# A fused RWKV, gated-attention and channel-mix kernel: stacked key halves for single heads, a weight split off TensorE, small steps on ScalarE, and another order

## The chip, the cores and the metric

The kernel runs on one core of one Trainium2 chip. Its time is the device time of one execution in microseconds (us); before the change the median of three runs is 636.58 us (636.41 to 636.62). A core has TensorE (PE in the profile, its weight loads PEld), VectorE (DVE), ScalarE (ACT), GpSimd (POOL) and SyncE (SP), which issues the DMAs. Each engine runs its own list of instructions in order, and the lists meet only at semaphores.

## The reference

Three layers in a row over 4 batches of 768 tokens, 384 wide, all in float32. Cut to what matters:

```python
# 1. RWKV recurrence, 8 heads of 48
y[t] = r[t] @ (state + outer(u * k[t], v[t]))
state = w[t][:, None] * state + outer(k[t], v[t])
# 2. four experts, each a causal attention with heads of 64; the two best experts of a token count
for e in range(4):
    q, k, v = x @ wq[e], x @ wk[e], x @ wv[e]
    a = softmax(where(causal, -1e9, (q @ k.T) / 8))
    out += gate[:, :, e] * (a @ v @ wo[e])
# 3. channel mix
out = x + relu(layernorm(x) * g_ln @ w_ch1) @ w_ch2
```

`wq` and `wk` are scaled by about 27, so that the scores are large and the products need more than float16.

## The kernel before

**Precision.** Matrices that TensorE multiplies are split into two float16 parts, a high one and a low one (value minus high). A product is three passes: high by high, high by low, low by high (`passes`, in the code a list of pairs). The split is made twice over in this kernel: ScalarE writes the high part (`q_hi`, `s_hi`, `hi`), then VectorE or, for weights, TensorE and ScalarE write the low part (`q_lo`, `s_lo`, `less` and `lo`).

**Stages.** A batch is 6 chunks of 128 tokens. `rwkv_chunk` computes the recurrence of a chunk by scans on VectorE and small float32 products on TensorE; its output goes transposed into the tiles `xT`, one for two chunks, five of them in turn (`SIZES`). `project` multiplies `xT` by the weights of queries and keys (`mm_q`, L1119; 12 results of a batch, each split by `q_hi` L1133 and `q_lo` L1139) and of values and gates (`mm_v`, L1175). `attend` goes over the 6 blocks of 128 queries: scores (`mm_s`, L1289, with a mask product at L1292), maximum (`s_max`, L1302 or L1307 and L1310), exponential (`s_exp`, L1325), split, transposing DMA, product with the values (`mm_av`, L1368), normalisation (`a_den`, L1381 to L1383), output projection (`mm_o`, L1416). Two blocks give 256 rows for `norm` and `mlp`: `mm_1` (L1509, 108 matmuls of 256 columns) and `mm_2` (L1542, 72 matmuls of 384 columns), 12 times in all.

**Scores.** A head has 64 rows, so queries and keys of an even head lie in rows 0 to 63 and those of an odd head in rows 64 to 127. Blocks 0 to 3 take two or four heads in one unit, and their 64-row matmuls of an even and an odd head run side by side. Blocks 4 and 5 (640 and 768 keys) take one head at a time (`alone`): 2 blocks, 4 heads and 4 batches make 32 such units. For these, four DMAs (`stack_q`, L1153) write a tile `xq` with the high part of the queries in one half of the rows and the low part in the other, and four (`stack_k`, L1161) a tile `xk` with the high part of the keys in both halves. One 128-row pass over `xq` and `xk` gives high by high plus low by high; a second, 64-row pass over `qs` and `kd` gives high by low. Each pass is two matmuls, of 512 columns and of the rest; the mask product of 128 columns and 128 rows closes the unit.

**Channel-mix weights.** `w1` and `w2` come as 12 parts of 384 columns each, `w2` in six loads of two parts. VectorE decodes a load (L501 to L503), ScalarE sums its squares (`top`, L571), and once the common scale is known TensorE multiplies a part by a diagonal of it (`times`, L651, float32), ScalarE takes the high part (L655), TensorE subtracts it in PSUM (`less`, L659) and ScalarE takes the rest (`lo`, L663). The loads of `w2` use the two slots of the ring `xnT`, which `top` frees; later the same slots hold the transposed input of `mm_1` (`n_tr`, L1481).

**Order.** A list scheduler (`Plan`) writes the instruction order of all engines when the kernel is built: at each step it takes, among the operations that could begin first, the one with the lowest due time; the due times are the table `PLACE` and `PRM`, and the operations' assumed durations stand in the decorators. The same scheduler places idle matmuls (`spin`) at the start.

Of the kernel before, what the change touches and what calls it, by code (L numbers as in the profile page):

```python
# [10 lines left out]
F16 = mybir.dt.float16  # L11
# [9 lines left out]
P = 128  # L21
# [16 lines left out]
PRM = dict(LOOK=0.0, LATE=47934.0429, UNTIL=42.7413, SPAN=5.8951, LEAST=0.3045, GAP=2.3171, LAND=3.0218, NPA=6, NCB=8, DIRECT=(), NST=10)  # L38
PLACE = {
# [21 lines left out]
    ('o', 3, 5): -870797.51, ('proj', 0): -59357.09, ('proj', 0, 's'): -132504.36, ('proj', 0, 1): 75985.76,  # L61
    ('proj', 0, 2): 89300.14, ('proj', 1): -94741.02, ('proj', 1, 1): -141865.08, ('proj', 1, 2): -157811.48,
    ('proj', 2): -48176.78, ('proj', 2, 1): 94543.45, ('proj', 2, 2): -181961.13, ('proj', 3): 107540.27,
# [12 lines left out]
    ('vals', 0, 1): 39151.57, ('vals', 0, 2): -75195.63, ('vals', 1): -80560.85, ('vals', 2): 73452.63,  # L76
# [7 lines left out]
    'a_den': 38701.56, 'a_hi': -195572.57, 'a_lo': 161429.85, 'a_of': -103979.76, 'a_tr': 60728.7, 'ae': -8236.41,  # L84
    'am_copy': 96077.58, 'f_flag': -50711.59, 'f_rows': 236752.87, 'f_turn': -27774.6, 'f_w': 1123.52,
    'forth': 199841.74, 'g_exp': 122945.11, 'g_norm': -163036.44, 'g_peak': -84778.11, 'g_rank': 193870.19,
    'hi': 120088.91, 'less': -59742.97, 'lo': -174825.96, 'load': -97454.62, 'load_g': -36209.35, 'load_k': 92145.76,
    'load_q': -162686.4, 'load_r': -200141.4, 'load_u': -146422.64, 'load_ut': -41677.41, 'load_v': 105043.21,
    'm_hi': -226505.89, 'm_lo': -64342.04, 'm_out': 50524.88, 'm_store': 131523.02, 'mk': 14805.25,
    'mk_begin': -11079.75, 'mk_bonus': -271559.55, 'mk_cb': -31506.68, 'mk_dec': -45642.9, 'mk_diag': -185610.32,  # L90
    'mk_k2': 219816.19, 'mk_k2t': 32281.43, 'mk_rk': -166425.51, 'mk_rp': -191192.09, 'mk_ruk': -73390.57,
    'mk_sd': -179119.84, 'mk_side': 127279.41, 'mk_tot': 151863.47, 'mm_1': 133873.4, 'mm_2': 142127.46,
    'mm_a': -13940.92, 'mm_av': -76739.24, 'mm_cb': -21123.48, 'mm_d': -92938.61, 'mm_inter': -14197.02,
    'mm_intra': -5176.94, 'mm_k': 70188.66, 'mm_o': 133574.61, 'mm_q': -86201.06, 'mm_s': -72808.96,
    'mm_v': -126599.75, 'mt': -8307.76, 'n_hi': -74748.1, 'n_lo': -150284.41, 'n_root': -142970.84, 'n_tr': 49369.16,
    'n_var': -25525.9, 'n_xn': -136866.98, 'o1': 107168.86, 'o2': -213807.54, 'o3': -34902.85, 'o4': -281533.5,
    'o5': 91577.3, 'o_mean': 175751.95, 'o_st': 105676.96, 'o_x1': -241637.87, 'q_hi': 157157.07, 'q_lo': -34330.46,
    's_exp': 45715.92, 's_hi': 108208.17, 's_lo': -37858.2, 's_max': 32187.35, 's_tr': 143781.36, 'scan': 175245.6,
    'se': -130347.73, 'stack_k': 55275.66, 'stack_q': 52291.37, 'state': -188149.3, 'times': 30753.27,
    'top': -21195.51, 'unpack': -224938.32, 'unpack2': 154504.25, 'unpack3': 177006.68, 'v_hi': 66433.51,  # L100
# [186 lines left out]


class _Op:
    pass  # L290


SIZES = dict(seq=2, bw=1, fw=2, rp=2, k2=2, tok=1, am=2, k2t=1, xT=5, vz=2, qs=1, kd=1, xq=1, xk=1,
             vt=1, ex=1, hl=2, pt=5, of=1, o16=2, oT=2, hid=8, x1=3, xnT=2, r=3, o=1, m=2, w=1)

PARTS = {0: ((0, 1), (2, 3), (4, 5))}

# [1436 lines left out]
```

## Time and profile before

| | |
|---|---|
| median of 3 runs | 636.58 us |
| the profiled execution | 637.08 us |
| its span, first to last instruction | 634.9 us |
| PE busy | 607.3 us, 96% |
| DVE busy | 437.5 us, 69% |
| ACT busy | 378.6 us, 60% |
| POOL busy | 141.2 us, 22% |

Busy time of an engine is the union of its instructions' records. A matmul's record reaches from its start to the end that the profile models, so that successive records overlap; what a matmul costs the engine is read from start to next start. The granted clock (PEclk) is a share of 2.4 GHz.

### The profile page before, as it was taken

To read this page: it belongs to the slowest core of one execution; us is meant where nothing else is said; L and a number is where in the kernel's file an instruction comes from. 1 tells how busy PE (TensorE), PEld (TensorE's weight loads), DVE (VectorE), ACT (ScalarE), POOL (GpSimd) and SP (SyncE) were. 2 spreads that over 40 slices of the span, in tenths; PEclk is the share of its full clock that TensorE was granted. 3 is DMA by queue.
4 is the path that set the end of the run, shared out by engine and by line. 5 is a ranking of instruction groups with operands and counts; after the bars stand their busy time and mean duration, and the time that the engine had idled before them with its cause. 6 is when DMAs were issued, how large, how long until landed. Compare 5 with 4: busy or idle time off the path is not lost.

```text
span 634.9 us, 16313 instructions
## 1 busy us (share of the span) xinstructions
PE 607.3 (96%) x6612; PEld 436.8 (69%) x6612; DVE 437.5 (69%) x861; ACT 378.6 (60%) x1008; POOL 141.2 (22%) x176
## 2 busy tenths in 40 slices
PE   5588999999999999999999999999999999999996
PEld 2454667677678767766787866766786767677783
DVE  6876789988688688889878366977556546453230
ACT  5287787956666856785757367565557646451320
POOL 4502034325434023343622001540000000000000
PEclk8589999999999999999999999999999999999999
DMA  8733645788674389788843537675306444532100
GB/s 272 258 96 122 208 102 148 149 198 169 160 200 107 52 170 214 174 202 180 193 122 61 115 55 163 151 163 105 65 10 147 87 101 75 120 56 59 38 14 30
DMA packets 148658, 81.10 MB, mean 128 GB/s; under 512 B 123616, under 2 KB 134624, under 8 KB 148576
## 3 DMA queue, kind: packets, MB, share of 16 engines
q1 hardware_dynamic: 148576, 79.98, 53.5%
q8 instruction: 54, 0.88, 0.6%
q14 instruction: 28, 0.23, 0.1%
HBM read 41.16 MB, written 4.72 MB: 72 GB/s over the span
## 4 chain that ended last, share of the span: by engine, by line
PE 81%; ACT 8%; DVE 7%; issue 2%; DMA 1%; SPq 1%; POOL 0%; ACTq 0%; DVEq 0%
PE pm L1509 22%; PE pz L1542 21%; PE pq L1119 6%; PE ps L1289 5%; PE po L1368 4%; PE pa L914 4%; PE px L1416 3%; PE py L964 3%; PE py L950 2%; PE pv L1175 2%; PE ps L1292 2%; PE pd L979 1%; PE pk L932 1%; PE w_ps_False L651 1%; DVE bw L797 1%
## 5 line engine op out<-in xcount | busy, mean ns | idle before, releaser
L1509 PE MATMUL pm<-xnT,w_w 128*128 128x256 f16 x1296 | 150.8, 273 | 1.2 <-ACT cb L854 0.9
L1542 PE MATMUL pz<-w_w,hid 128*128 128x384 f16 x864 | 151.2, 326 | 0.0
L1509 PEld LDWEIGHTS <-w_w 128*128 128x128 f16 x1296 | 125.0, 98 | 18.7 <-issue 2.6
L1542 PEld LDWEIGHTS <-hid 128*128 128x128 f16 x864 | 81.6, 98 | 49.9 <-issue 1.6
L1520 ACT ACTIVATE hid<-pm 128x512 f16<-128x512 f32 x72 | 42.8, 594 | 56.1 <-PE pm L1509 55.7
L1524 DVE SCALAR_TENSOR_TENSOR hid<-pm,hid 128x512 f16<-128x512 f32 x72 | 49.4, 686 | 38.8 <-ACT hid L1520 38.5
L1345 DVE SCALAR_TENSOR_TENSOR hl<-ps,hl 128x512 f16<-128x512 f32 (+2 forms) x68 | 54.9, 811 | 25.8 <-ACT hl L1341 25.1
L1458 POOL TENSOR_TENSOR rs_y<-rs_v,half 128x2 f32<-128x2 f32 x12 | 8.4, 700 | 215.1 <-ACT rs_v L1454 215.1
L887 POOL TENSOR_SCALAR_AFFINE_SELECT am<-cb 128x512 f32<-128x512 f32 x48 | 37.9, 813 | 77.8 <-DVE cb L873 43.3
L1119 PE MATMUL pq<-xT,w_qk 128*128 128x256 f16 x432 | 52.3, 273 | 0.5 <-DVE qs L1139 0.4
L1341 ACT ACTIVATE hl<-ps 128x512 f16<-128x512 f32 (+2 forms) x68 | 46.9, 696 | 1.1 <-DVE hl L1345 0.3
L1325 ACT ACTIVATE ps<-ps,bias,scales 128x128 f32<-128x128 f32 (+3 forms) x64 | 37.8, 591 | 15.5 <-DVE bias L1310 12.4
L1119 PEld LDWEIGHTS <-w_qk 128*128 128x128 f16 x432 | 41.2, 98 | 8.3 <-issue 1.9
L1325 ACT ACTIVATE ps<-ps,bias 128x640 f32<-128x640 f32 (+1 forms) x32 | 26.2, 820 | 34.6 <-DVE ps L1302 33.1
L829 POOL TENSOR_TENSOR rp<-seq,fw 128x512 f32<-128x512 f32 x24 | 30.0, 1249 | 61.7 <-DVE fw L812 57.7
L1302 DVE TENSOR_SCALAR_CACHE_REDUCE ps<-ps,scales 128x640 f32<-128x640 f32 (+1 forms) x32 | 30.6, 956 | 16.9 <-PE ps L1292 16.8
L1368 PEld LDWEIGHTS <-pt 128*128 128x128 f16 x1008 | 36.8, 98 | 5.1 <-issue 1.4
L1368 PE MATMUL po<-vt,pt 128*128 128x64 f16 x1008 | 39.9, 193 | 0.0
L921 DVE COPY_PREDICATED am<-above,pa 128x512 f32<-128x512 int8 x48 | 33.4, 724 | 5.0 <-PE pa L914 3.3
L797 DVE TENSOR_TENSOR_SCAN bw<-seq,starts 128x516 f32<-128x516 f32 x24 | 32.6, 1360 | 2.4 <-DMA seq<-in_seq_dram 2.4
L1289 PE MATMUL ps<-kd,qs 64*128 64x512 f16 (+3 forms) x256 | 32.9, 303 | 0.5 <-DVE hl L1345 0.5
L1307 DVE TENSOR_REDUCE top<-ps 128x2 f32<-128x512 f32 (+3 forms) x28 | 25.5, 912 | 10.5 <-PE ps L1292 10.5
(214 smaller groups left out, 1044.7 us busy)
## 6 DMA issues: line engine op xcount, KB each, us to landing
seq<-in_seq_dram SPq DMA_DIRECT2D x48, 256.0 KB, 4.3
seq<-in_seq_dram SPq DMA_DIRECT2D x24, 258.5 KB, 3.4
tok<-in_tok_dram SPq DMA_DIRECT2D x16, 384.0 KB, 3.8
seq<-in_seq_dram SPq DMA_DIRECT2D x24, 192.0 KB, 4.7
xnT<-in_w_dram SPq DMA_DIRECT2D x6, 768.0 KB, 5.0
x<-in_w_dram SPq DMA_DIRECT2D x4, 1152.0 KB, 7.1
out_dram<-x SPq DMA_DIRECT2D x24, 192.0 KB, 2.7
xk<-kd SPq DMA_DIRECT2D x16, 192.0 KB, 3.6
```

Of the source, the lines that this page charges most:

```text
L797: V.tensor_tensor_scan(t["bw"][:, NP * CW : 0 : -1], t["wT"][:, NP * CW : 0 : -1], starts[:, NP * CW : 0 : -1], 0.0, op0=OP.mult, op1=OP.max)
L887: G.affine_select(out=t["am"][:, j], in_=t["cb"].rearrange("p (h j) -> p h j", j=2)[:, :, j, None].to_broadcast([P, NP, P]), compare_op=OP ...
L1119: T.matmul(h["pq"][:, :n].rearrange("p (c t) -> p c t", t=P), wt["qk"][:, lw, kk, mt * P : (mt + 1) * P], t["xT", c0 // 2][:, :, lx * KK + ...
L1289: T.matmul(h["all"][:, at_ : at_ + k1 - k0], q, k, start=at_ // 512 not in begun, stop=False, skip_group_check=True)
L1325: A.activation(ps, ps, AF.Exp, bias=h["bias"][:, e : e + 1], scale=-1.0 if alone else t["x"]["esc"], accum_out=r["sums"][:, e : e + 1])
L1341: A.activation(part(u, heads, 0, W), view(heads, h, W, spot), AF.Copy, scale=2.0 ** 14)
L1345: V.scalar_tensor_tensor(out=part(u, heads, half_at, W), in0=view(heads, h, W, spot), scalar=2.0 ** 14, in1=part(u, heads, 0, W), op0=OP.m ...
L1368: T.matmul(r["po"][:, e * HD : (e + 1) * HD], u["pt"][:, (lp * len(heads) + k) * (i + 1) + kb, :], t["vt"][:, kb, lv, e * HD : (e + 1) * H ...
L1509: T.matmul(h["pm"][:, j * 256 : (j + 1) * 256].rearrange("p (c t) -> p c t", t=P), wt["w1"][:, 4 * kk + f // 3, lw, f % 3 * P : (f % 3 + 1 ...
L1520: A.activation(hid[fp][:, 0], h["pm"], AF.Relu)
L1524: V.scalar_tensor_tensor(out=hid[fp][:, 1], in0=h["pm"], scalar=0.0, in1=hid[fp][:, 0], op0=OP.max, op1=OP.subtract)
L1542: T.matmul(h["po"][:, :DM], hid[fp][:, lh, c0 : c0 + P], wt["w2"][:, 2 * fp + j, lw, :], start=(fp + j + i == 0), stop=(fp == NF // 2 - 1 ...
```

## The change

Six things change.

- For single heads `xk` now holds the high part of the keys in one half of the rows and the low part in the other, and `xq` holds two copies of the queries: the high part in both halves, and the low part in both halves. Both passes read `xq` and `xk` with 128 rows, and the product low by low is added. The number of matmuls and their columns are the same.
- `w2` becomes DIRECT for its last five loads (10 of 12 parts): no `times` and no `less`. ScalarE writes the high part from the decoded raw tile with the scale, and VectorE subtracts it (`lo`); the slots of `xnT` are freed by `lo`.
- In batch 0 the low part of queries and keys (`q_lo`) is made by TensorE (`q_less`, a product with the diagonal `minus15`) and ScalarE in place of VectorE.
- The bias of the exponential in units of two or four heads (`s_bias`) and the first step of `a_den` (`a_sum`) go from VectorE to ScalarE.
- `xT` has four tiles in place of five; the assumed cost of some operations changes, and `top` gets four buffers.
- `PRM` and every entry of `PLACE` are new, so every engine's order is.

```diff
-PRM = dict(LOOK=0.0, LATE=47934.0429, UNTIL=42.7413, SPAN=5.8951, LEAST=0.3045, GAP=2.3171, LAND=3.0218, NPA=6, NCB=8, DIRECT=(), NST=10)
+PRM = dict(LOOK=0.0, LATE=1773.6262, UNTIL=43.8356, SPAN=6.2999, LEAST=0.0732, GAP=2.1085, LAND=2.27, NPA=6, NQ=1, NCB=8, DIRECT=('w2',), NST=10)
...
+            if b < PRM["NQ"]:
+                @op("PE", n / 2400 + 0.01, after=[q_hi])
+                def q_less(tag=tag, m=m, h=h, cols=cols, n=n):
+                    T.matmul(h["pq"][:, :n], minus15, t[tag][:, m, 0, cols], start=False, stop=True, skip_group_check=True)
+
+                @op("A", n * 0.83e-3 + 0.17, after=[q_less], follow=[lo_before], free=[ak])
+                def q_lo(tag=tag, m=m, h=h, cols=cols, n=n):
+                    A.activation(t[tag][:, m, 1, cols], h["pq"][:, :n], AF.Copy, scale=2.0 ** -15)
...
-                for rows, lq in ((a, 0), (o, 1)):
-                    nc.sync.dma_start(t["xq"][rows, j::2], t["qs"][a, :, lq, 4 * P :])
+                for rows in (a, o):
+                    nc.sync.dma_start(t["xq"][rows, j], t["qs"][a, :, :, 4 * P :])
...
-                for rows in (a, o):
-                    nc.sync.dma_start(t["xk"][rows, j::2], t["kd"][a, :, 0])
+                for rows, lk in ((a, 0), (o, 1)):
+                    nc.sync.dma_start(t["xk"][rows, j::2], t["kd"][a, :, lk])
...
-                    for lq, lk in ((2, 2), (0, 1)) if alone else passes:
+                    for lq, lk in ((0, 2), (1, 2)) if alone else passes:
...
-                        if lq == 2:
-                            q, k = t["xq"][:, e, (i - 4) * P : (i - 3) * P], t["xk"][:, e, k0:k1]
+                        if lk == 2:
+                            q, k = t["xq"][:, e % 2, e // 2, lq, (i - 4) * P : (i - 3) * P], t["xk"][:, e, k0:k1]
...
-                    V.tensor_scalar(bias, top, t["x"]["nesc"], None, op0=OP.mult)
+                        A.activation(bias, h["top"], AF.Copy, scale=t["x"]["nesc"])
...
+            @op("A", 0.21, after=exps)
+            def a_sum(r=r, nm=nm):
+                r["den"] = small("den", [P, E], f"den_{nm}")
+                A.activation(r["den"], r["sums"], AF.Copy, scale=2.0 ** 14, bias=1e-9 * 2.0 ** 14)
```

The code that DIRECT turns on is in the kernel before, unused there (L621 to L637 of the function `big_weights`).

## Rows read from the trace of the kernel before

**Rows 1.** The page, part 1: busy us, share of the span, instructions.
```profile
PE 607.3 (96%) x6612; PEld 436.8 (69%) x6612; DVE 437.5 (69%) x861; ACT 378.6 (60%) x1008; POOL 141.2 (22%) x176
```

**Rows 2.** Stretches: length, busy PE, PEld, DVE, ACT, POOL, granted clock, DMA share, GB/s.
```profile
0.00:36.00 36.00, 22.06 (x167) 13.57 (x170) 27.85 (x72) 17.54 (x64) 15.22 (x28) 0.67 0.72 236
36.00:128.00 92.00, 85.20 (x874) 56.48 (x865) 76.46 (x148) 76.06 (x222) 25.26 (x29) 1.00 0.52 142
128.00:320.00 192.00, 191.96 (x2483) 141.19 (x2485) 159.68 (x295) 127.54 (x333) 69.93 (x80) 1.00 0.74 167
320.00:512.00 192.00, 191.07 (x2101) 141.31 (x2094) 127.85 (x270) 115.32 (x304) 29.00 (x37) 1.00 0.48 103
```

**Rows 3.** The page, part 4: the chain that ended last, by engine.
```profile
PE 81%; ACT 8%; DVE 7%; issue 2%; DMA 1%; SPq 1%; POOL 0%; ACTq 0%; DVEq 0%
```

**Rows 4.** PE's timeline, one single-head unit of 640 keys: start, us, instructions.
```profile
405.38 0.43 PE L1289 MATMUL ps<-xk,xq 128*128 128x512 f16 x2
405.75 0.44 PE L1289 MATMUL ps<-kd,qs 64*128 64x512 f16 x2
406.12 0.23 PE L1292 MATMUL ps<-neg,ident 128*128 128x128 bf16 x1
```

**Rows 5.** The chain in order of time: start, us, engine, line, instructions.
```profile
205.67 1.99 PE pv L1175 x18
...
353.31 11.79 PE pm L1509 x108
```

**Rows 6.** Instructions of L1289: weight loads of `xq`, ns min/median/max, first and last start.
```profile
L1289 PEld LDWEIGHTS <-xq x64: 95/98/99, 142.9 to 568.2; 128*128 128x128 f16 x64
```

**Rows 7.** SP's timeline: the four loads of `xq` of batch 0.
```profile
124.00 2.72 SPq L1153 DMA_DIRECT2D xq<-qs  x4
```

**Rows 8.** PE's timeline around parts of w2 and a `less`: start, us, instructions.
```profile
100.36 0.33 PE L659 MATMUL w_ps_False<-w_w,minus 128*128 128x384 f16 x1
100.53 0.49 PE L1119 MATMUL pq<-xT,w_qk 128*128 128x256 f16 x3
...
102.18 1.46 PE L651 MATMUL w_ps_False<-w_w,diag 128*128 128x384 f32 x4
103.47 0.49 PE L1119 MATMUL pq<-xT,w_qk 128*128 128x256 f16 x3
```

**Rows 9.** Groups by line and shape: busy us, mean ns, idle before, its releasers.
```profile
L663 ACT ACTIVATE w_w<-w_ps_False 128x384 f16<-128x384 f32 x24 | 11.5, 492 | 4.7 <-PE w_ps_False L659 4.6
L1139 DVE SCALAR_TENSOR_TENSOR qs<-pq,qs 128x256 f16<-128x256 f32 x24 | 9.7, 420 | 5.0 <-ACT qs L1133 4.7
L1133 ACT ACTIVATE kd<-pq 128x256 f16<-128x256 f32 x24 | 9.2, 388 | 3.8 <-PE pq L1119 3.8
L503 DVE SCALAR_TENSOR_TENSOR w_w<-xnT,w_w 128x768 int32<-128x768 int32 x6 | 6.7, 1113 | 0.1
L1071 DVE SCALAR_TENSOR_TENSOR xT<-py,scales,xT 128x384 f16<-128x384 f32 x24 | 14.7, 611 | 2.7 <-ACT xT L1067 2.4
L1310 DVE TENSOR_SCALAR bias<-top,scales 128x2 f32<-128x2 f32 x24 | 5.5, 228 | 0.8
L1433 ACT ACTIVATE mv<-mv 128x1 f32<-128x1 f32 x24 | 4.9, 203 | 0.4
```

**Rows 10.** ACT's timeline: batch 2's third chunk goes into `xT`.
```profile
263.01 0.57 ACT L1067 ACTIVATE xT<-py,scales 128x384 f16<-128x384 f32 x1
```

**Rows 11.** Timeline from the fifth load of `w2` to the first `mm_1`.
```profile
100.16 0.89 ACT L571 ACTIVATE xnT<-w_w 128x768 f32<-128x768 f32 x1
...
101.16 0.35 SPq L548 DMA_DIRECT2D xnT<-in_w_dram  x1
...
119.80 0.85 ACT L571 ACTIVATE xnT<-w_w 128x768 f32<-128x768 f32 x1
...
120.97 2.94 SPq L1481 DMA_TRANSPOSE xnT<-x  x1
...
127.28 1.14 PE L1509 MATMUL pm<-xnT,w_w 128*128 128x256 f16 x9 [0.91 <-ACT cb L854]
```

More of the change, by code (lines that the diff above doesn't have):

```diff
@@ L290 @@
     pass
-SIZES = dict(seq=2, bw=1, fw=2, rp=2, k2=2, tok=1, am=2, k2t=1, xT=5, vz=2, qs=1, kd=1, xq=1, xk=1,
+SIZES = dict(seq=2, bw=1, fw=2, rp=2, k2=2, tok=1, am=2, k2t=1, xT=4, vz=2, qs=1, kd=1, xq=1, xk=1,
              vt=1, ex=1, hl=2, pt=5, of=1, o16=2, oT=2, hid=8, x1=3, xnT=2, r=3, o=1, m=2, w=1)
@@ L407 @@
     V.tensor_scalar(minus, ident, -1.0, None, op0=OP.mult)
+    minus15 = const.tile([P, P], F16, name="minus15")
+    V.tensor_scalar(minus15, ident, -(2.0 ** 15), None, op0=OP.mult)
     spare = const.tile([P, DM], F8, name="spare")
@@ L1135, in project, with q_lo @@
             hi_before = q_hi
-            @op("V", n * 1.04e-3 + 0.16, after=[q_hi], follow=[lo_before], free=[ak])
-            def q_lo(tag=tag, m=m, h=h, cols=cols, n=n):
-                V.scalar_tensor_tensor(out=t[tag][:, m, 1, cols], in0=h["pq"][:, :n], scalar=2.0 ** -15,
-                                       in1=t[tag][:, m, 0, cols], op0=OP.mult, op1=OP.subtract)
+            if b < PRM["NQ"]:
[5 more added lines that the diff above has]
+                    A.activation(t[tag][:, m, 1, cols], h["pq"][:, :n], AF.Copy, scale=2.0 ** -15)
+            else:
+                @op("V", n * 1.04e-3 + 0.16, after=[q_hi], follow=[lo_before], free=[ak])
+                def q_lo(tag=tag, m=m, h=h, cols=cols, n=n):
+                    V.scalar_tensor_tensor(out=t[tag][:, m, 1, cols], in0=h["pq"][:, :n], scalar=2.0 ** -15,
+                                           in1=t[tag][:, m, 0, cols], op0=OP.mult, op1=OP.subtract)
             lo_before = q_lo
@@ L1145, in project @@
         plan.at("proj", b, 2)
-        @op("SP", 1.75, after=lows[8:10], dma=(2.7, 0.8), take=[("xq", b)])
+        @op("SP", 1.75, after=lows[8:10], dma=(2.7, 1.6), take=[("xq", b)])
         def stack_q():
-            t["xq"] = buf("xq", [P, E, 2 * P], F16, f"xq_{b}")
+            t["xq"] = buf("xq", [P, 2, E // 2, 2, 2 * P], F16, f"xq_{b}")
             for j in range(2):
                 a, o = slice(64 * j, 64 * j + 64), slice(64 - 64 * j, 128 - 64 * j)
-                for rows, lq in ((a, 0), (o, 1)):
-                    nc.sync.dma_start(t["xq"][rows, j::2], t["qs"][a, :, lq, 4 * P :])
+                for rows in (a, o):
+                    nc.sync.dma_start(t["xq"][rows, j], t["qs"][a, :, :, 4 * P :])
         @op("SP", 1.75, after=lows[2:4] + lows[6:8] + lows[10:12], dma=(2.7, 2.4), take=[("xk", b)])
@@ L1272, in attend @@
                     pair = [e for e in unit if e // 2 == m]
-                    for lq, lk in ((2, 2), (0, 1)) if alone else passes:
+                    for lq, lk in ((0, 2), (1, 2)) if alone else passes:
                         todo += [(e, lq, lk, k0, k1) for k0, k1 in pieces for e in pair]
-                busy = ((2 if alone else 1.5) * W + P) * len(unit) / 2400 + 0.13
+                busy = ((2 if alone else 1.5) * W + P) * len(unit) / 2400 + (0.04 if alone else 0.13)
                 @op("PE", busy, dense=0.8, after=pr["lows"][: 4 * (i // 2 + 1)] + (pr["stacks"] if alone else []), follow=[before_ps, pr["mv"][i // 2 * 2 + 1]], take=aks,
@@ L1295, in attend @@
                 me["s"].append(mm_s)
-                busy_v = W * 1.042e-3 + 0.25 if alone else len(unit) * W * 1.042e-3 + 0.31
+                busy_v = W * 1.042e-3 + 0.23 if alone else len(unit) * W * 1.042e-3 + 0.25
                 @op("V", busy_v, after=[mm_s, t["x"]["rest"]])
                 def s_max(unit=unit, h=h, nm=nm, W=W, spot=spot):
-                    h["bias"] = small("bias", [P, E], f"bias_{nm}_{unit[0]}", 4)
                     if len(unit) == 1:
+                        h["bias"] = small("bias", [P, E], f"bias_{nm}_{unit[0]}", 4)
                         V.tensor_scalar(h["all"][:, :W], h["all"][:, :W], t["x"]["nesc"], 3.0e38,
@@ L1305, in s_max, with s_bias @@
                     k = len(unit) // 2
-                    top = small("top", [P, 2, k], f"top_{nm}_{unit[0]}", 2)
+                    top = h["top"] = small("top", [P, 2, k], f"top_{nm}_{unit[0]}", 4)
                     V.tensor_reduce(out=top, in_=h["all"].rearrange("p (j x) -> p j x", x=512)[:, :, : k * W].rearrange("p j (q w) -> p j q w", w=W),
                                     axis=AX.X, op=OP.max)
-                    bias = h["bias"][:, unit[0] : unit[0] + 2 * k].rearrange("p (q j) -> p j q", j=2)
-                    V.tensor_scalar(bias, top, t["x"]["nesc"], None, op0=OP.mult)
+                s_bias = None
+                if not alone:
+                    @op("A", 0.21, after=[s_max])
+                    def s_bias(unit=unit, h=h, nm=nm):
+                        h["bias"] = small("bias", [P, E], f"bias_{nm}_{unit[0]}", 4)
+                        bias = h["bias"][:, unit[0] : unit[0] + len(unit)].rearrange("p (q j) -> p j q", j=2)
+                        A.activation(bias, h["top"], AF.Copy, scale=t["x"]["nesc"])
                 for heads in shelves:
@@ L1317, in attend @@
                     half_at = n * W
-                    @op("A", n * (W * 0.833e-3 + (0.32, 0.4, 0, 0.43)[n - 1]), after=[s_max])
+                    @op("A", n * (W * 0.833e-3 + (0.32, 0.4, 0, 0.43)[n - 1]), after=[s_bias or s_max])
                     def s_exp(heads=heads, h=h, nm=nm, r=r, W=W, spot=spot, alone=alone):
@@ L1376, in attend @@
             me["av"].append(before_av)
-            @op("V", 0.6, pair=True, after=exps + [pr["gates"][pr["part"][i]]])
+            @op("A", 0.21, after=exps)
+            def a_sum(r=r, nm=nm):
+                r["den"] = small("den", [P, E], f"den_{nm}")
+                A.activation(r["den"], r["sums"], AF.Copy, scale=2.0 ** 14, bias=1e-9 * 2.0 ** 14)
+            @op("V", 0.4, pair=True, after=[a_sum, pr["gates"][pr["part"][i]]])
             def a_den(i=i, r=r, nm=nm):
-                den = r["den"] = small("den", [P, E], f"den_{nm}")
-                V.tensor_scalar(den, r["sums"], 2.0 ** 14, 1e-9 * 2.0 ** 14, op0=OP.mult, op1=OP.add)
+                den = r["den"]
                 V.reciprocal(den, den)
```

50 lines of the change are left out of this document (26 added, 24 removed), and 80 rows, old and new, of the table PLACE.

## The prediction

> **What bounds the kernel now.** I read the page's busy shares first: TensorE is busy 96% of the span, VectorE 69%, ScalarE 60% [rows 1]. A share is an average, so next I read the busy time by stretch [rows 2]. From 128 us on TensorE has work in 191.96 of 192 and, up to 512 us, 191.07 of 192 us; VectorE reaches at most 159.68 of 192 there. TensorE's stream is the bound, and a microsecond taken out of it is a microsecond off the end. From 36 to 128 us it is nearly so: PE 85.20 of 92, with DVE at 76.46 and ACT at 76.06 close behind. Only the first 36 us are something else: PE has 22.06, at a mean granted clock of 0.67, and waits for loads and for VectorE. The chain that ended last agrees: 81% of it is PE [rows 3]. What the change takes from TensorE after 128 us therefore counts in full; what it takes between 36 and 128 us counts until another engine is late.
>
> **Single heads.** I go by start to next start. A unit of 640 keys starts its 128-row pass at 405.38, its 64-row pass at 405.75 and its mask product at 406.12: 0.37 us for each pass [rows 4]. What the columns alone need comes from `mm_1`: 108 matmuls of 256 columns in 11.79 us are 109 ns each, 0.426 ns a column [rows 5], so 640 columns need 0.273 us. Each pass thus has 0.10 us over, once where the rows go from 128 to 64 and once on the way back. After the change both passes and the mask product have 128 rows, so both are gone: 0.2 us a unit (0.37 + 0.37 less 2 x 0.273 is 0.194), and I take the same for the 768-key units, whose number of switches is the same. 32 units x 0.194 = 6.2 us, all after 128 us, whatever the order, since a unit begins and ends with 128 rows before and after. Columns and matmuls stay as many; the product low by low lies in rows that were empty.
>
> The rows show no cost of a weight load of the full rows behind a matmul of the full rows: each of those 109 ns matmuls has its own weight load, and a load of the full rows lasts 98 ns [rows 6]; one behind the other they would be over 200. The Trainium skill says otherwise: TensorE: Matmul & The Clock Gate, Part 3, "The mechanism", holds that a weight load overlaps a running matmul only where its row group differs, and every load of the new passes has all row groups. By that rule the gain of this part would go (first rival); the trace disagrees with 109 ns.
>
> The loads of `xq` double in bytes. Those of batch 0 are issued from 124.00 on [rows 7], its first unit begins at 142.9 [rows 6]: 18 us cover them, so I cost them at nothing. Without cover the price is the length of the four issues again, at most 2.7 us a batch.
>
> **The second channel-mix weight.** Two parts of `w2` in float32 take from 102.18 to 103.47, 0.645 us a part, and a `less` from 100.36 to 100.53, 0.17 us [rows 8]. Ten parts: 8.2 us off TensorE. `q_less` adds 12 matmuls of 256 columns, 12 x 0.109 = 1.3 us. A wait of TensorE for the high part stands in front of each subtraction before and after; ten go and twelve come, so I leave that at zero, between a gain of 1 and a cost of 1 us. Net on TensorE: 6.9 us, nearly all between 36 and 128 us.
>
> How much of it counts depends on the others in that stretch. ScalarE loses ten `lo` of 0.492 (4.9) and gains twelve `q_lo` of 0.388 (4.7) and its small steps [rows 9]: about six `s_bias` and four `a_sum` at 0.203, 2.0 us; the high part of a weight costs the same from either memory, as far as the rows tell. VectorE loses twelve `q_lo` of 0.420 (5.0) and those ten small steps at 0.228 (2.3), and gains ten `lo`: nothing in the trace reads that tile for a subtraction, and the nearest rows are L503, which reads the same raw tile (1113 ns for 768 elements, 0.56 a part), and L1071, the same operation on 384 elements from PSUM (0.61). I take 0.56, the same source: 5.6 us. So in this stretch PE goes from 85.2 to 78.3, ACT from 76.1 to 77.9, DVE from 76.5 to 74.8. If all 6.9 us came off the stretch, it would be 85.1 us long with ACT busy 92% of it and PE 92%. Today one engine alone reaches 93% there [rows 2], and the three hand work to each other in small pieces, so I do not believe in two at once. If half comes off, 88.5 us, both stand at 88%. I take half: 3.5 us.
>
> **The rest.** The small steps moved to ScalarE (28 biases, 24 sums) take some 12 us from VectorE and give ScalarE about 11; after 128 us VectorE is at most 83% busy and ScalarE 66% [rows 2], so both are worth nothing by themselves. `a_sum` puts a hop into `a_den`, which waits for the exponentials of the block, while the product with the values comes later still. `xT` with four tiles: a pair of chunks waits for the pair four before it. In the trace the closest meeting is batch 2's second pair, first written at 263.01 [rows 10], and batch 1's first pair, whose last reader `mm_v` is over at 207.7 [rows 5]: 55 us of cover, worth nothing. The new order moves every queue. It cannot change the sum of columns, but the number of switches between row or column shapes outside the single-head units; at 0.10 us each, fifteen more or fewer are 1.5 us either way, which I keep for the range.
>
> **The sum.** 6.2 + 3.5 = 9.7 us. The profiled execution took 637.08 with a span of 634.9, so it would take 627.4; it stands 0.5 above the median of the runs, 636.58, so the median goes to 626.9.
>
> **The rivals.**
> - Weight loads of full rows are exposed. Two loads of a second pass cost 98 ns each, what the two switches cost, so the 6.2 us are lost and only 3.5 remain: 633.1. Against it are the 109 ns above. Chance 0.02.
> - The whole 6.9 us of the weights count, as VectorE's relief lets the order fill TensorE: 6.2 + 6.9 = 13.1, 623.5. For it: VectorE has 15 us free in the stretch. Against it: ACT at 92%. Chance 0.22.
> - None of it counts. The first `mm_1`, at 127.28 [rows 11], stays where it is, and TensorE waits in front of it for what it saved: 6.2 alone, 630.4. For it: the sixth load of `w2` is issued at 101.16, when the square of the fifth, from 100.16 on, is done, and the transpose that `mm_1` needs goes at 120.97, when the square of the sixth is done [rows 11]. The slots of `xnT` are in the way there today. Chance 0.17.
> - The same slots, worse: the kernel gets slower. A load's slots are now held past the square for two `hi` (0.49 each) and two `lo` (0.56 each), 2.1 us. If the five loads follow one another without a gap, the first `mm_1` comes 5 x 2.1 = 10.5 us later, at 137.8. With TensorE's work before it 6.9 us less, it waits 17.4 us more than now; less the 13.1 saved that is 4.3 us slower: 640.9. It decides from 133.5 on, where the delay of 6.2 eats the single heads' gain. Against it: before the fifth load they are not back to back, six loads being spread over 100 us. Chance 0.05.
> - The first stretch stays at the lower clock for longer, since the idle matmuls are placed anew: the mean of 0.67 to 36 us is time at 1.2 GHz, then 2.4 GHz to the end of the work [rows 2]. Each further microsecond at 1.2 GHz costs half a one; ten more give back 5 us: 631.9. Chance 0.04.
> - My forecast, half of the weights' gain and all of the single heads': 626.9. Chance 0.5.
>
> **How the numbers follow.** The likeliest is 626.9. The range goes from 622.0 (all of it, and fifteen switches fewer) to 631.5 (none of it, and ten switches more), which leaves out the two smallest rivals on the far side. 0.2% of this kernel is 1.3 us, about what a measurement can tell from no change. Only the slot rival ends slower: 0.05. Within 1.3 us needs the none-of-it case together with a worse order: 0.03. Faster: 0.92.
>
> **What would show it.** In the trace after: a single-head unit takes 0.6 us from its first matmul to the end of the mask product in place of 0.8, with no idle weight queue inside; no L651 with `diag` but for two parts; PE in 36 to 128 us at 85 to 90% instead of 93%, and ACT the engine that is late there; the first `mm_1` between 120 and 127 us; from then on PE without gaps, so that the time from it to the end is shorter by some 6 us. If the stretch from the first `mm_1` to the end is not shorter, the single-head step is wrong; if `mm_1` is not earlier, the half is wrong; if the first `mm_1` is after 133.5, the sign is.

## The result, and the profile after

The changed kernel takes 629.52 us in the median of four runs (628.8 to 630.5), the kernel before 636.60 in four runs (636.41 to 637.87): a ratio of 0.9886, 95% interval 0.9867 to 0.9904. It is 7.1 us faster. The forecast was 626.9, so the time lies inside the range, and 2.6 of the 9.7 us did not come. The profiled execution took 629.59 with a span of 627.3, against 637.08 and 634.9.

Parts 1 and 4 of the page after (compare [rows 1] and [rows 3]):

```profile
PE 598.3 (95%) x6593; PEld 440.9 (70%) x6594; DVE 427.4 (68%) x808; ACT 386.0 (62%) x1062; POOL 140.1 (22%) x176
...
PE 72%; ACT 12%; DVE 10%; issue 3%; DMA 2%; SPq 0%; POOL 0%; ACTq 0%; DVEq 0%
```

TensorE has 9.0 us less to do (607.3 to 598.3), more than the time that was won. And of the chain that ended last, ScalarE now holds 12% in place of 8, VectorE 10 in place of 7. The stretches of after, with the columns of [rows 2]:

```profile
0.00:36.00 36.00, 23.52 (x161) 14.49 (x164) 28.70 (x71) 16.91 (x61) 18.71 (x29) 0.68 0.71 236
36.00:128.00 92.00, 83.11 (x903) 57.13 (x902) 77.26 (x143) 78.86 (x237) 27.23 (x29) 0.94 0.54 143
128.00:320.00 192.00, 190.45 (x2504) 143.91 (x2502) 160.36 (x280) 130.07 (x354) 73.64 (x87) 1.00 0.79 173
320.00:512.00 192.00, 191.13 (x2101) 143.61 (x2090) 120.69 (x249) 123.08 (x334) 18.71 (x28) 1.00 0.53 108
```

Cut at the first `mm_1` instead, before and then after, same columns:

```profile
0.00:127.28 127.28, 106.54 (x1027) 69.41 (x1027) 103.63 (x216) 92.88 (x284) 39.78 (x55) 0.91 0.58 169
127.28:628.96 501.68, 500.71 (x5586) 367.40 (x5585) 333.21 (x645) 285.71 (x725) 101.40 (x121) 1.00 0.54 118
```
```profile
0.00:128.10 128.10, 106.73 (x1060) 71.72 (x1062) 105.96 (x213) 95.88 (x297) 46.05 (x58) 0.87 0.59 169
128.10:622.10 494.00, 491.57 (x5535) 369.15 (x5532) 320.83 (x594) 290.08 (x766) 94.02 (x119) 1.00 0.57 122
```

So the accounting of the spans is: the first `mm_1` comes 0.8 us **later** (127.28 to 128.10), the stretch from it to the end of the last `mm_2` is 7.7 us shorter (501.68 to 494.00), the tail behind it 0.7 shorter (634.9 less 628.96 is 5.9, 627.3 less 622.10 is 5.2). Everything that was won was won behind the first `mm_1`, where the single heads lie; in front of it, where `w2` lies, no time was won. The two stretches do not hold quite the same work: some 2.6 us of TensorE's work on one further chunk now stands in front of the first `mm_1` (counted in the section on the prediction).

**Three sizes.** A single-head unit of 640 keys, from TensorE's timeline (compare [rows 4]):

```profile
406.48 0.71 PE L1302 MATMUL ps<-xk,xq 128*128 128x512 f16 x4
407.03 0.22 PE L1305 MATMUL ps<-neg,ident 128*128 128x128 bf16 x1
```

From the first matmul to the mask product 0.55 us, before 0.74 (406.12 less 405.38): 0.19 less, as worked out. And the steps that were new to their engine, groups by line and shape with the columns of [rows 9]:

```profile
L659 ACT ACTIVATE w_w<-w_ps_False 128x384 f16<-128x384 f32 x14 | 6.9, 505 | 2.7 <-PE w_ps_False L655 1.3 <-DVE w_w L506 0.8 <-PE py L954 0.7
...
L636 DVE SCALAR_TENSOR_TENSOR w_w<-xnT,s_all_False,w_w 128x384 f16<-128x384 f32 x10 | 6.8, 708 | 1.5 <-ACT w_w L632 1.4
L632 ACT ACTIVATE w_w<-xnT,s_all_False 128x384 f16<-128x384 f32 x10 | 6.2, 651 | 0.0
...
L1329 ACT ACTIVATE bias<-top,scales 128x2 f32<-128x2 f32 x24 | 7.1, 295 | 15.3 <-DVE top L1320 15.1
L1400 ACT ACTIVATE den<-sums 128x4 f32<-128x4 f32 x24 | 5.0, 208 | 0.0
...
L1071 ACT ACTIVATE xT<-py,scales 128x384 f16<-128x384 f32 x24 | 14.0, 583 | 0.0
```

A low part from the raw tile costs VectorE 0.71 us in the mean (0.56 taken), a high part from it ScalarE 0.65 (from PSUM 0.505 without a scale, L659, and 0.583 with a scale for each row, L1071; the high part from the raw tile has such a scale), an `s_bias` on ScalarE 0.295 (0.203 taken), an `a_sum` 0.208 (0.203 taken). The row of L1329 also shows ScalarE idle for 15.1 us in all until VectorE's maximum `top` (L1320) is there. Most of that wait was there before, one step later, when the exponential waited for the bias from VectorE; before and after, total us, times, longest:

```profile
ACT ps L1325 <- DVE bias L1310: 12.4, 13, 3.4
```
```profile
ACT bias L1329 <- DVE top L1320: 15.4, 10, 3.3
```

### The profile page after: what moved, and what is told of

Same layout as the page of the kernel before. It is cut to its first block, busy times and chain, and to the rows that moved or that the text cites. A ratio compares the mean times of both kernels' runs of the same rounds, so it can differ in the third digit from the quotient of the medians.

```text
span 627.3 us, 16254 instructions
## 1 busy us (share of the span) xinstructions
PE 598.3 (95%) x6593; PEld 440.9 (70%) x6594; DVE 427.4 (68%) x808; ACT 386.0 (62%) x1062; POOL 140.1 (22%) x176
## 4 chain that ended last, share of the span: by engine, by line
PE 72%; ACT 12%; DVE 10%; issue 3%; DMA 2%; SPq 0%; POOL 0%; ACTq 0%; DVEq 0%
PE pz L1565 21%; PE pm L1532 18%; PE pq L1123 7%; PE ps L1302 5%; PE po L1387 4%; PE px L1439 3%; ACT ps L1344 3%; PE pa L918 3%; PE py L968 2%; PE py L954 2%; PE pv L1188 1%; PE pk L936 1%; ACT hl L1360 1%; PE pd L983 1%; DMA xnT<-in_w_dram 1%
## 5 line engine op out<-in xcount | busy, mean ns | idle before, releaser
L891 POOL TENSOR_SCALAR_AFFINE_SELECT am<-cb 128x512 f32<-128x512 f32 x48 | 34.7, 745 | 40.2 <-DVE cb L877 26.2
L1572 DVE SCALAR_TENSOR_TENSOR x<-pz,ioutFalse,x 128x384 f32<-128x384 f32 x24 | 14.7, 614 | 36.7 <-PE pz L1565 36.7
L801 DVE TENSOR_TENSOR_SCAN bw<-seq,starts 128x516 f32<-128x516 f32 x24 | 30.9, 1288 | 1.5 <-DMA seq<-in_seq_dram 1.5
L918 PE MATMUL pa<-rp,k 48*128 48x128 f32 x384 | 29.6, 290 | 1.7 <-DVE dec L996 1.6
```

Source lines behind the costliest of these rows:

```text
L891: G.affine_select(out=t["am"][:, j], in_=t["cb"].rearrange("p (h j) -> p h j", j=2)[:, :, j, None].to_broadcast([P, NP, P]), compare_op=OP ...
L918: T.matmul(t["pa"][j][:, hp * P : (hp + 1) * P], t["k2"][o : o + D, hp, :], t["rp"][o : o + D, hp, :], start=True, stop=True)
```

## The experiments

Two questions: are the 7 us the single heads alone, and why did TensorE's relief in front of the first `mm_1` bring nothing? In all runs but two (the weight's step alone, and undone) every engine's order is that of the kernel that they are made from. "First `mm_1`" is read from the row of its line in the profiled execution: count, ns min/median/max, first and last start. The time between first and last start then measures the second stretch.

### The single heads alone, and everything but them

The first is the kernel before with the change of `xq`, `xk` and the passes only (and four tiles `xT`, to make room); its order is that of before.

```diff
-                for rows, lq in ((a, 0), (o, 1)):
-                    nc.sync.dma_start(t["xq"][rows, j::2], t["qs"][a, :, lq, 4 * P :])
+                for rows in (a, o):
+                    nc.sync.dma_start(t["xq"][rows, j], t["qs"][a, :, :, 4 * P :])
...
-                    for lq, lk in ((2, 2), (0, 1)) if alone else passes:
+                    for lq, lk in ((0, 2), (1, 2)) if alone else passes:
```

> The kernel before with the single heads' edit alone (xk high over low, xq twice, both passes of 128 rows; xT with four tiles so that xq fits); every engine keeps the order of before, and only the rows of 64 matmuls and the contents of two tiles change. Theory A (the 64 switches of rows cost 0.097 us each, and TensorE's stream is the bound after 128 us): 636.6 - 6.2 = 630.4, with a unit of 640 keys from first matmul to mask product in 0.55 us in place of 0.74. Rival 1 (weight loads of the full rows are exposed, 98 ns each, in place of the switches): 636.6, units as long as before. Rival 2 (the gain is given back in later waits, since VectorE or ScalarE must feed the faster stream): 632 to 635, with new idle time of PE after 128 us.

Measured: 631.03 against 637.31, ratio 0.9895 (0.9879 to 0.991), 6.3 us. The second is the changed kernel with the same edit taken back, in the changed kernel's order.

> The changed kernel with the single heads' edit alone undone, every engine's order as in the changed kernel. Theory A: 629.5 + 6.2 = 635.7, so that the rest of the change is worth no more than 1 us. Rival (the edit is worth something only in one of the two orders): 629.5 to 632, the remaining 4 to 7 us then coming from the weights and the order.

Measured: 636.16 against 637.31, ratio 0.9984 (0.997 to 0.9998). So without the single heads the whole rest of the change is worth 1.0 us (0.0016 of 637; 0.1 to 1.9 by the interval). The rows of `mm_1` in before, in the heads alone, in everything but the heads, and in after:

```profile
L1509 PE MATMUL pm<-xnT,w_w x1296: 269/273/283, 127.3 to 617.0; 128*128 128x256 f16 x186
```
```profile
L1509 PE MATMUL pm<-xnT,w_w x1296: 270/273/283, 128.4 to 612.1; 128*128 128x256 f16 x186
```
```profile
L1532 PE MATMUL pm<-xnT,w_w x1296: 270/273/283, 128.0 to 615.8; 128*128 128x256 f16 x186
```
```profile
L1532 PE MATMUL pm<-xnT,w_w x1296: 269/273/283, 128.1 to 610.1; 128*128 128x256 f16 x186
```

From first to last start: 489.7 before, 483.7 with the heads alone, 487.8 with all but the heads, 482.0 after. The heads are 6.0 of it in the old order and 5.8 in the new, and they are the same whatever stands in front. TensorE's switches between different numbers of rows or columns behind the first `mm_1`, counted in the traces, go from 219 to 155 with the heads alone: 64 fewer for 6.3 us of the median, 0.098 us each. The unit of 640 keys of that run:

```profile
415.68 0.71 PE L1289 MATMUL ps<-xk,xq 128*128 128x512 f16 x4
416.22 0.22 PE L1292 MATMUL ps<-neg,ident 128*128 128x128 bf16 x1
```

0.54 us, so no weight load of the full rows shows between the matmuls. The Trainium skill says in one sentence of TensorE: Matmul & The Clock Gate, Part 3, "The mechanism", that a weight load overlaps running matmuls only where its row group differs, which would leave the loads of the new passes exposed; the same section also says that a load into the background weight buffer is pulled ahead. These rows and the 6.3 us show no exposed load, and the measurement decides.

### The weight's step alone, and undone

One constant each: the changed kernel without the new way for `w2`, and the kernel before with it.

```diff
-PRM = dict(LOOK=0.0, LATE=1773.6262, ..., DIRECT=('w2',), NST=10)
+PRM = dict(LOOK=0.0, LATE=1773.6262, ..., DIRECT=(), NST=10)
```

> The changed kernel with the split of the second channel-mix weight back on TensorE (DIRECT empty), the table of due times unchanged: TensorE has 8.2 us more before the first mm_1, VectorE 6.8 us less (ten subtractions of 0.708 us), ScalarE 6.2 less and 9.9 more. Theory B (the stretch from 36 us to the first mm_1 is held by VectorE and ScalarE as much as by TensorE, so the weights' gain did not count): 629.5 to 632. Rival (TensorE alone holds it, and the gain was lost to something else, such as the clock or the new order): 637.

> The kernel before with the split of the second weight on ScalarE and VectorE alone (DIRECT for w2), with the old table of due times. Theory B: 635 to 639, as VectorE has 6.8 us more in a stretch where it is 83% busy. Rival (TensorE alone holds the stretch): 636.6 - 8.2 = 628.4.

Measured: 673.3 (ratio 1.0563, 1.0549 to 1.0577) and 664.2 (1.0429, 1.0413 to 1.0445). Both are far from what either theory gave. The row of `mm_1` says why, the first kernel and then the second:

```profile
L1532 PE MATMUL pm<-xnT,w_w x1296: 269/273/421, 191.5 to 651.9; 128*128 128x256 f16 x186
```
```profile
L1509 PE MATMUL pm<-xnT,w_w x1296: 269/273/283, 166.5 to 639.9; 128*128 128x256 f16 x186
```

With other operations the scheduler writes another order for all engines, since the due times in `PLACE` fit one set of operations: the first `mm_1` comes 63 and 39 us later. This tells that the due times go with the operations, and nothing of the weight's step itself. A version of it alone in a held order was not tried.

### More and less work for one engine in front of the first `mm_1`

So the question was put in another way: in the changed kernel, order held, each engine gets some 7 us more, or less, between 36 and 128 us. More: `lo` twice (VectorE), `hi` twice (ScalarE), the first matmul of the queries and keys of batch 0 seven times (TensorE).

```diff
-                        V.scalar_tensor_tensor(out=wt[which][:, part, 1], ...
+                        for _ in range(2): V.scalar_tensor_tensor(out=wt[which][:, part, 1], ...
```
```diff
-                        A.activation(wt[which][:, part, 0], ...
+                        for _ in range(2): A.activation(wt[which][:, part, 0], ...
```
```diff
-                        T.matmul(h["pq"][:, :n]...
+                        for more in range(6 if b == 0 and kk + i == 0 else 0, -1, -1): T.matmul(h["pq"][:, :n]...
```

> The changed kernel, every engine's order held, with each of the ten VectorE subtractions of w2 issued twice (0.708 us each in the trace of the changed kernel, so 7.1 us of VectorE more before the first mm_1). Theory B (VectorE, ScalarE and TensorE hold the stretch before the first mm_1 together): 2 to 5 us slower, 632 to 634.5, the first mm_1 later by as much. TensorE alone: 629.5. VectorE alone: 636.6.

> The same with each of the ten high parts of w2 on ScalarE issued twice (0.651 us each, 6.5 us more). Theory B: 2 to 4 us slower, 631.5 to 633.5. TensorE alone or VectorE alone: 629.5 to 630. ScalarE alone: 636.

> The same with the first matmul of each of batch 0's twelve query and key results issued seven times (72 matmuls of 256 columns more, 0.109 us each, 7.9 us of TensorE before the first mm_1; each starts its sum anew). It puts back on TensorE about what the weights' split took off. Theory B: 3 to 6 us slower, 632.5 to 635.5. TensorE alone: 637.4. If TensorE had all of it to spare: 629.5.

Less: `lo` left out, `mm_2` reading the high part in its place (VectorE); the exponential with a sum at L822 left out for nine chunks (ScalarE); only the high by high pass of queries and keys in batch 0 (TensorE); and all three together.

```diff
-                    for i, (lw, lx) in enumerate(passes):
+                    for i, (lw, lx) in enumerate(passes[:1] if b == 0 else passes):
```
```diff
-                        V.scalar_tensor_tensor(out=wt[which][:, part, 1], ...
+                        if False: V.scalar_tensor_tensor(out=wt[which][:, part, 1], ...
```
```diff
-            A.activation(w, w, AF.Exp, scale=20.0, ...
+            if n > 8: A.activation(w, w, AF.Exp, scale=20.0, ...
```

> The changed kernel, order held, with the two low passes of batch 0's queries and keys left out (72 matmuls, 7.9 us less on TensorE before the first mm_1; batch 0's scores are computed with the high parts alone). Theory B: 0 to 3 us faster, 626.5 to 629.5, since the two other engines set when the next operand is there. TensorE alone: 621.6.

> The changed kernel, every engine's order held, with the ten VectorE subtractions of w2 left out (7.1 us less of VectorE before the first mm_1; the channel mix reads the high part of those rows in place of the low). What is known by now: 7 us more on VectorE, ScalarE or TensorE each moved the first mm_1 later by 5.4 to 6.6 us, and 7.9 us less on TensorE did not move it. If VectorE is what holds the stretch: the first mm_1 at about 122 and 623 us. If a chain through all three does: 0 to 3 us faster, 626.5 to 629.5.

> The same with the check of the decay (0.72 and 0.20 us on ScalarE) left out for the first nine chunks, seven of which come before the first mm_1: 6.4 us less of ScalarE there. If ScalarE holds the stretch: 623. If a chain through all three does: 0 to 3 us faster.

> The three reliefs together: no subtraction of w2 on VectorE, no check of the decay for nine chunks on ScalarE, only the high pass of batch 0's queries and keys on TensorE. If the three engines hold the stretch together, the first mm_1 comes 4 to 7 us earlier than with any one alone: 622 to 626. If something else holds it (the loads, POOL, or the order itself): 628 to 630, as with each alone.

| run | median, us | ratio to before | 95% interval | first `mm_1` | last `top` ends | between |
|---|---|---|---|---|---|---|
| after | 629.52 | 0.9886 | 0.9867 to 0.9904 | 128.10 | 125.07 | 3.0 |
| 7.1 more, VectorE | 637.08 | 1.001 | 0.9988 to 1.0032 | 134.74 | 131.72 | 3.0 |
| 6.5 more, ScalarE | 635.66 | 0.9989 | 0.9969 to 1.0009 | 133.46 | 130.15 | 3.3 |
| 7.9 more, TensorE | 636.78 | 1.0008 | 0.9989 to 1.0028 | 133.82 | 129.41 | 4.4 |
| 7.9 less, TensorE | 631.07 | 0.9905 | 0.9876 to 0.9935 | 128.30 | 125.27 | 3.0 |
| 7.1 less, VectorE | 629.06 | 0.987 | 0.9845 to 0.9895 | 130.41 | 127.11 | 3.3 |
| 6.4 less, ScalarE | 628.63 | 0.9879 | 0.9862 to 0.9895 | 125.83 | 122.80 | 3.0 |
| less of all three | 627.63 | 0.9849 | 0.982 to 0.9878 | 124.16 | 121.13 | 3.0 |

(`top` is L1320 on VectorE, start plus duration of its row; differences of under 2 us between the medians of this table are inside the intervals. The last three columns are from one profiled execution of each kernel. At 37 us, where the edits on `w2` and on batch 0's products have touched nothing yet, the executions of these runs already lie 0.3 to 1.0 us in front of that of after, so a difference of 1 to 2 us in these columns says little.)

More work on any of the three costs 6 to 8 us, about all that was added. That is outside the 2 to 6 us of theory B; each run came out as forecast for the case that its engine alone holds the stretch. But less work on one of them brings nothing that the intervals can tell, so none of them holds it alone. In particular 7.9 us less on TensorE, more than the 6.9 net that the prediction counted for `w2`, move the first `mm_1` by nothing. Nor do the three together set all of it: with some 21 us less on them the first `mm_1` comes only 3.9 us earlier, and 627.63 lies between the two forecasts for that run (622 to 626, and 628 to 630). What else holds the stretch (the loads, POOL, the order) was not taken apart.

The last links of the run with 7.9 us less on TensorE, rows of VectorE's, ScalarE's and TensorE's timelines (idle time before and its releaser in brackets):

```profile
124.05 1.22 DVE L1320 TENSOR_REDUCE top<-ps 128x2 f32<-128x1024 f32 x1
...
125.30 0.30 ACT L1329 ACTIVATE bias<-top,scales 128x2 f32<-128x2 f32 x1 [1.71 <-DVE top L1320]
125.63 0.75 ACT L1344 ACTIVATE ps<-ps,bias,scales 128x512 f32<-128x512 f32 x1
...
127.30 0.37 ACT L1137 ACTIVATE kd<-pq 128x256 f16<-128x256 f32 x1
...
127.72 0.27 PE L1144 MATMUL pq<-kd,minus 128*128 128x256 f16 x1 [2.51 <-ACT kd L1137]
127.83 0.62 PE L936 MATMUL pk<-ident,k 128*128 128x128 f32 x4
128.30 4.78 PE L1532 MATMUL pm<-xnT,w_w 128*128 128x256 f16 x27
```

VectorE's maximum ends at 125.27. ScalarE, idle for 1.71 us, takes the bias, then the exponentials, then the high part of a key tile. TensorE, idle for 2.51 us, takes `q_less` of that tile, and `mm_1` stands behind it in TensorE's order. Two of these links came with the change: `s_bias` on ScalarE, and `q_less` on TensorE. A second thing ends there at the same time: the transpose `n_tr`, which `mm_1` reads, goes only at 122.65 and lands 5.6 us later, at 128.26, 0.04 us before `mm_1` starts.

```profile
122.65 1.43 SPq L1504 DMA_TRANSPOSE xnT<-x  x1
...
DMA to landing us min/median/max: 5.6/5.6/5.6
```

And the idle time is paid for again. Behind it the granted clock falls, from 1.00 to 0.50 (from 2.4 to 1.2 GHz), and the first 27 matmuls of `mm_1` take 4.78 us, against 3.11 in the changed kernel: 1.7 us, about what this run's median lies above after's. Stretches of 2 us in the run with 7.9 us less on TensorE:

```profile
128.00:130.00 2.00, 2.00 (x14) 1.57 (x13) 0.78 (x2) 2.00 (x7) 0.32 (x1) 0.66 1.00 240
130.00:132.00 2.00, 2.00 (x11) 1.42 (x10) 1.55 (x3) 1.47 (x4) 0.00 (x0) 0.50 0.92 308
```

In the changed kernel itself:

```profile
121.92 1.14 DVE L636 SCALAR_TENSOR_TENSOR w_w<-xnT,s_all_False,w_w 128x384 f16<-128x384 f32 x2
...
123.85 1.22 DVE L1320 TENSOR_REDUCE top<-ps 128x2 f32<-128x1024 f32 x1
...
127.11 0.37 ACT L1137 ACTIVATE kd<-pq 128x256 f16<-128x256 f32 x1
...
127.53 0.27 PE L1144 MATMUL pq<-kd,minus 128*128 128x256 f16 x1
127.64 0.62 PE L936 MATMUL pk<-ident,k 128*128 128x128 f32 x4
128.10 3.11 PE L1532 MATMUL pm<-xnT,w_w 128*128 128x256 f16 x27
```

It is the same chain at the same distance, 3.03 us from the end of `top` to `mm_1`, only that TensorE has just enough work not to stand idle in front of it. In the table that distance is 3.0 to 3.3 us in all runs but the one with more work on TensorE. And VectorE has no room in front of `top`. Its stretches from 114.40 to `top`, first after, then 7.9 us less on TensorE (columns of [rows 2]):

```profile
114.40:125.10 10.70, 9.92 (x91) 7.88 (x92) 10.32 (x28) 8.86 (x27) 3.13 (x4) 0.84 0.72 144
```
```profile
114.40:125.30 10.90, 9.51 (x122) 7.08 (x121) 10.55 (x27) 8.49 (x26) 3.07 (x4) 0.84 0.61 151
```

10.32 of 10.70 us and 10.55 of 10.90. So at the end of the stretch it is VectorE's queue that sets the first `mm_1`, and TensorE's relief becomes 2.51 us of idle time there. That VectorE's work alone isn't the whole of it shows in the run with 7.1 us less on it: its `top` is not earlier. That it is 2 us later belongs to the one profiled execution (630.64, the slowest of four): its lateness against after arises between 46 and 57 us, with the clock at 0.50 from 44 to 48 us (after: 1.00), and from 57 to 118 us, where six of the ten subtractions are left out, the run gains nothing on after. Further in front the chain goes through all three engines; which links hold it there was not taken apart.

### More idle matmuls at the start

The changed kernel's granted clock is lower than before's between 36 and 128 us, 0.94 against 1.00: it is at 0.50 up to 44.0 us (before: up to 36.4), and again from 115.7 to 119.1, behind a wait of TensorE for VectorE of 1.58 us. To test the clock, eight idle matmuls of 256 columns went behind each of two small transposes near the start, order held.

```diff
-            T.transpose(t["ps"][:n, :P], t["cm"], ident)
+            T.transpose(t["ps"][:n, :P], t["cm"], ident); [T.matmul(t["ps"][:, 256:512], ident16, starts[:, :256], start=True, stop=True) for _ in range(8)]
```

> The changed kernel, every engine's order held, with eight idle matmuls of 256 columns put behind each of the two transposes that the scales need (at 25 and 28 us, where TensorE waits 2.7 us). In the profile of the changed kernel TensorE was at 1.2 GHz from 26.9 to 44.0 us, 7.6 us longer than before. Theory C (the lower clock in the first stretch is no loss, since TensorE waits there anyway): 628.5 to 630.5, whatever the clock does. Rival (the longer time at 1.2 GHz took half a microsecond for each, and is why the weights' gain is missing): up to 3.8 us faster, 625.7 to 627, if the clock rises earlier.

Measured: 633.0, ratio 0.9953 (0.9936 to 0.997), 3.5 us over the changed kernel, the first `mm_1` at 131.52. Neither expectation holds. What the run shows is a delay: the idle matmuls put off the product of the scales behind them, 32.93 in place of 31.11, and the 1.8 us late there are 3.4 late at `mm_1`. The clock did not come earlier: it is at 0.50 from 44 to 48 us, where after has 1.00.

The window of the first 36 us seems to say the opposite (0.88, in after 0.68), but it can't be read so. The records of the clock begin at 24.3 us in this run and at 6.4 in after, and what lies in front of them counts as 1.00. The stretch from 12 to 18 us and six idle matmuls in it, first this run, then after:

```profile
12.00:18.00 6.00, 4.26 (x11) 0.80 (x12) 3.80 (x4) 3.86 (x20) 3.34 (x4) 1.00 0.96 358
...
12.63 3.78 PE L744 MATMUL spin<-starts,ident 128*128 128x512 bf16 x6 [0.50 <-PE pcb L853]
```
```profile
12.00:18.00 6.00, 3.78 (x9) 0.77 (x12) 2.86 (x4) 4.86 (x25) 2.34 (x3) 0.50 1.00 363
...
12.70 3.79 PE L744 MATMUL spin<-starts,ident 128*128 128x512 bf16 x6 [0.50 <-PE pcb L853]
```

The same matmuls take the same time under 1.00 and under 0.50. So mean clocks over a span, which include this stretch, can't be compared between executions either. What can be compared is the stretch behind 36 us. In the runs with more on VectorE and with less on ScalarE the clock rises to 1.00 at 38.2 us, in after at 44.0. Their VectorE is 1.0 and 1.2 us in front of after's at the decode that starts at 37.45 in after, and 2.2 and 2.4 us at the chunk that it writes to `xT` at 45.80, for which it waits 1.35 and 1.36 us where after waits 2.56. By this comparison the later rise cost after's profiled execution about 1.2 us. It also explains the run with less on ScalarE: all of the 2.3 us by which its first `mm_1` comes earlier is there by 46 us, and the run with more on VectorE, which has no relief, had as much at that point. How often the clock rises late, and so what it does to the median, no run shows.

## Why the prediction was right, and where it was wrong

- **What bounds the kernel.** Right behind 128 us: 491.57 of 494.00 us busy, and what came out of the stream there came off the end. "What it takes between 36 and 128 us counts until another engine is late" was right as a sentence; how near that point was, was misread (below).
- **Single heads, 6.2 us, whatever the order.** Right: 6.3 alone in the old order, 6.2 by the ratios (0.9984 less 0.9886) or 6.6 by the medians (636.16 less 629.52) in the new, 0.19 us a unit as worked out. The rival of the exposed weight loads is refuted by the same runs.
- **The weight off TensorE, half of 6.9 us.** This is the step that failed. 3.5 us were forecast. All of the change but the single heads, the weight among it, measured 1.0. The first `mm_1` was forecast between 120 and 127 us and came at 128.10; by the prediction's own sentence the half is wrong. "Half" came from asking at what length of the stretch no engine would be above 88% busy. That is a share of a stretch again, the reading that the first paragraph warned of. What ends the stretch is a chain through three queues, and in the changed kernel's order TensorE, though the busiest, is no link that can be shortened: 7.9 us less on it bring nothing, 7.9 us more cost 7. In before, too, TensorE stood idle for 0.91 us in front of the first `mm_1`, waiting for ScalarE [rows 11]. The rival "none of it counts", 630.4, is nearest to the time; that 629.52 lies in the range is owed to the single heads and to a range wide enough for that rival. What `w2`'s step alone is worth was not measured.
- **Its reason** named the slots of `xnT`. In before the row of 120.97 did not show that they were in the way: the square of the sixth load ends at 120.65, but the input of the transpose `n_tr` is ready only at 120.72, and SP's issue in front of it ends at 120.85. After the change they are in the way, once: VectorE's last two `lo` end at 123.06 and `n_tr`, which needs their slot, goes at 123.08, though its input was ready at 116.81. It lands at 126.78, 1.3 us before `mm_1`, which in this run waits for the chain through `top`. Where TensorE had less to do, `n_tr` went at 122.65, landed at 128.26, and the two ended together: with the chain any shorter the transpose would have held `mm_1` back. So the rival's mechanism is there as a second limit, close behind the first, and not five times over. The rows of after:

```profile
115.86 0.95 DVE L1497 TENSOR_TENSOR x<-xn,x 128x768 f16<-128x768 f32 x1
...
123.08 1.43 SPq L1504 DMA_TRANSPOSE xnT<-x  x1
```

- **Engines in 36 to 128 us.** Forecast PE 78.3, ACT 77.9, DVE 74.8; measured 83.11, 78.86, 77.26. TensorE's number has two things in it that were not forecast: some 2.6 us of work of one further chunk that now stands in front of `mm_1` (16, 32 and 4 more matmuls of three kinds), and the lower clock, 0.94. VectorE's has that chunk and the larger `lo` in it. "ACT the engine that is late there" was right of the waits in front of TensorE, but its last one goes back to VectorE.
- **Sizes of single steps.** `lo` 0.71 for 0.56, `hi` from the raw tile 0.65 for 0.49, `s_bias` 0.295 for 0.203. Together 1.5, 1.6 and, for six biases, 0.6 us on two engines with no room: small, but all of one sign. For `hi` the prediction took the row without a scale; [rows 10] had a ScalarE step of the same size with one, 0.57.
- **Small steps "worth nothing by themselves".** Right behind 128 us, where TensorE has no gaps; not in front, where `s_bias` and `q_less` are links of the chain.
- **The order, 1.5 us either way.** It took away five switches behind the first `mm_1` beyond the 64 (219 to 150), 0.5 us, and moved the chunk. With 1.5 us more of idle time behind `mm_1` (501.68 less 500.71 is 1.0, 494.00 less 491.57 is 2.4), these make 1.6 of the 1.9 us by which the second stretch of all but the heads is shorter than before's.
- **The clock rival** came true in part. The clock rose at 44.0 us in place of 36.4. At the rival's price, half a microsecond for each, 7.6 us would cost 3.8; the traces above show about 1.2 us for the 5.8 us between 38.2 and 44.0. What the second fall (115.7 to 119.1) cost is not shown. How much of the missing 2.6 us is the clock's stays open.
- **The range** was said to leave out the two smallest rivals. It leaves out three: 631.9, 633.1 and 640.9, with a chance of 0.11 together.

What stays open: which links set the chain between 36 and 114 us, what else holds the first `mm_1` when all three engines have less to do, and whether `w2`'s step pays in an order made for it. An order in which VectorE's eleven small gate steps between 120.90 and 123.94 (about 1.9 us busy) come behind `top` would be the next thing to try; it was not.

## What to carry to other kernels

Where TensorE has no gap, a price read from start to next start can be multiplied by its count: here 0.10 us for each change of rows, 64 times, was the gain in either order. Where three in-order engines are each above 80% busy, do not share a saving out by percentages: follow the instruction that ends the stretch back through the queues, look for a second chain that ends close behind it, and count a saving only if its engine is a link. Here work added anywhere cost nearly its full length, and work taken from one engine brought nothing. And before a mean clock is compared, check the duration of one matmul that both runs have.

## What the runs showed of the hardware

- A change of the rows between TensorE's matmuls costs 0.10 us: 64 fewer, 6.3 us.
- A ScalarE step on 384 float32 values takes 0.505 us from PSUM without a scale (L659), 0.583 from PSUM with a scale for each row (L1071), and 0.651 with such a scale from every second word of an SBUF tile (L632). VectorE's subtraction from the same tile takes 0.61 us in the median and up to 1.21, against 0.61 from PSUM [rows 9].
- Behind 2.51 us of waiting the granted clock fell to 0.50 (128.6 to 132.0 us), and the first 27 matmuls of `mm_1` took 4.78 us; at 1.00 they take 3.11.
- A granted clock of 1.00 near the start can stand for missing records: six idle matmuls take 3.78 us under 1.00 and 3.79 under 0.50.
